# The first weight load of a cached-attention kernel as two transfers (16 rows and 112) instead of one of 128

## The chip, the cores and the metric

One core of a Trainium2 chip runs the whole kernel. The metric is device time in microseconds for one execution. The kernel before was timed in three runs: 678.33, 678.34 and 678.43 us, median 678.34 us.

## The reference

One decoding step for 8 sequences of width 512. The input is layer-normed; attention with 32 query heads over 8 cached key/value heads of 4096 positions gives `s`, and a gated MLP gives `g`; the result is `x + s * silu(g)`. Cut to what matters:

```python
xn = _layernorm(x)                                   # 8 x 1 x 512
q = (xn @ wq).reshape(B, 1, 32, 128)                 # wq: 512 x 4096
scores = einsum("bhqd,bhkd->bhqk", q, k) * 128**-0.5 # k_cache, v_cache: 8 x 8 x 4096 x 128
s = einsum("bhqk,bhkd->bhqd", softmax(scores), v) @ wo
z = gelu(xn @ w_in); z1, z2 = halves of z
g = silu((z1 * (w_sp * _layernorm(z2) + b_sp)) @ w_out)
return x + s * g
```

Everything is float32. The two caches are 134 MB each, wq and wo 8.4 MB each, and every byte is read once.

## The kernel before, in words

The on-chip memory holds three large slots, `slot_a`, `slot_b` and `slot_c`. Each has 128 rows (partitions) of 64 KB: 8.39 MB. Nearly all data passes through them in whole-slot transfers, and the host has laid out every array so that row p of a slot is one contiguous run of 64 KB in main memory.

All loads are issued by one engine's queue, SyncE (SP), in program order, and run in that order on the core's 16 DMA engines:

- In `prologue`: wq into `slot_b` (L96), x into a corner of `slot_c` (L103, 8 rows of 2 KB), the MLP's weights `w_mlp` into the rest of `slot_c` (L104, 128 rows of 42 KB), and the first half of head 0's keys, `kT[0, 0]`, into `slot_a` (L105). None of these four waits for anything. Then, when the q products have read wq, the second half of the keys goes into `slot_b` (L161).
- In `Heads.loads`, for each of the 8 key/value heads: values' first half into `slot_c` (L278), values' second half into `slot_b` (L280), the next head's keys' first half into `slot_a` (L283) and second half into `slot_b` (L276). Each waits until TensorE has read what the slot held. After the last head, wo comes into `slot_a` in seven pieces that are all 128 rows high and ever narrower (L285), and at last the rows of x for the final sum (L286).

The prologue's compute starts with the layer norm of x (L136 to L140), its transposition (L143, L144), and the q products with wq (64 matmuls, L151), for which both x and wq must have landed. The MLP follows (L164 to L224). Its transfers and engines are ordered by a scheduling framework, which adds the waits: an operation that reads a slot waits for each transfer that wrote the part it reads, and the load at L161 waits both for wq's landing and for the matmuls that read it.

In `Heads` the waits are written by hand with semaphores. `head_products` is TensorE's program, a loop over the heads: scores for the keys in `slot_a` and `slot_b` (L358), a few small products for the softmax, then the products with the values in `slot_c` and `slot_b` (L380). `head_sides` is what VectorE and ScalarE do beside it: maximum, exponentials, transposition, sums. `last_products` and `last_sides` multiply by wo (L415, L424, L437) as its pieces land, multiply by the gate and add x (L264), and ScalarE stores the result (L335).

Of the kernel before, what the change touches and what calls it, by code (L numbers as in the profile page):

```python
# [33 lines left out]
STEPS = 8  # L34
WARM = 384
AHEAD_OF_V = 11


class Chip:
# [52 lines left out]
def prologue(tc, t, x, w_mlp, wq, k0, k1, landed_a, landed_b):  # L92

    nc = tc.nc
    slot_a, slot_b, slot_c = t.slots
    nc.sync.dma_start(slot_b, wq)  # L96
    wq_sb = slot_b.rearrange("p (k n) -> p k n", k=NK)
    w_in_sb = slot_c[:, :N_IN].rearrange("p (k n) -> p k n", k=NK)
    w_out_sb = slot_c[:, N_IN:N_IN + N_OUT].rearrange("p (j d) -> p j d", j=NB)
# [131 lines left out]
class Heads:  # L231
# [116 lines left out]
    def head_products(self):  # L348
# [20 lines left out]
        for half, (slot, landed) in enumerate(((slot_c, self.landed_c), (slot_b, self.landed_b))):  # L369
            if half:  # L370
                flat = t.pT.rearrange("p j b g r -> p (j b g r)")
                with nc.tensor.Fori(0, AHEAD_OF_V):
                    nc.tensor.matmul(t.scr[1], t.ident, flat[:, :512], start=True, stop=True)  # L373
# [74 lines left out]
def gqa_gmlp_decode(nc, x, kT, v, wq, wo, w_mlp, x_rows, out):  # L448
    t = Chip(nc)
    landed_a, landed_b, stored = (nc.alloc_semaphore(s) for s in ("landed_a", "landed_b", "stored"))  # L450
    with tile.TileContext(nc) as tc:
        prologue(tc, t, x, w_mlp, wq, kT[0, 0], kT[0, 1], landed_a, landed_b)
    heads = Heads(nc, t, landed_a, landed_b, stored)
    heads.loads(kT, v, wo, x_rows)
    for h in range(HKV):
        heads.head_sides(h)
    heads.last_sides(out)
    nc.sync.wait_ge(stored, 16).then_inc(stored, -16)
    with nc.tensor.Fori(0, HKV):
        heads.head_products()  # L460
    heads.last_products()
# [39 lines left out]
```

## Time and profile before

| | |
|---|---|
| median of three runs | 678.34 us |
| profiled execution | 678.71 us, span 677.4 us |
| TensorE matmul busy | 405.8 us (60%) |
| VectorE busy | 80.0 us (12%) |
| DMA | 290.89 MB, mean 429 GB/s over the span |
| mean granted TensorE clock | 0.816 |

The profile is of one execution. Its span runs from the first to the last instruction; the profiled execution's own time is a little longer, and lies 0.37 us above the median. A row of a group or an issue names the line of the kernel, the engine, the tile written and the tile read. "SPq" is the queue of SyncE, which issues the loads. For an issue, the last number is the time until the data has landed. In the forty slices, DMA is the busy share of the 16 DMA engines in tenths.

### The profile page before, as it was taken

The page shows a single profiled execution, that of the slowest core. Times are in us where ns is not written, and L with a number is a line of the kernel's source. Part 1 is how long each engine was busy: PE and PEld are TensorE (multiplying, and loading weights), DVE is VectorE, ACT ScalarE, POOL GpSimd, SP SyncE. Part 2 cuts the span into 40 slices and gives each one's busy share as a digit, 9 for nine tenths or more (in the row PEclk, how much of TensorE's full clock was granted, in tenths as well). Part 3 has the DMA queues.
Part 4 walks back from the last instruction along what each step waited for, and adds up shares of the span by engine and source line. Part 5 has one row for each costly group of instructions (what it writes and reads, how often), then busy time and mean ns, then how long its engine had stood idle before and what let it go on. Part 6 is the DMA issues. An engine that isn't in the chain of part 4 may idle for free. (4 is left out here: it accounts for less than half of the span.)

```text
span 677.4 us, 5930 instructions
## 1 busy us (share of the span) xinstructions
PE 405.8 (60%) x2660; PEld 133.2 (20%) x2660; DVE 80.0 (12%) x157; ACT 13.8 (2%) x28; POOL 2.8 (0%) x15
## 2 busy tenths in 40 slices
PE   0446749346875449445794349555593349655598
PEld 0112213111221113111231113111131013211134
DVE  0142021102110021102110021101100021100211
ACT  0010000000000000000000000000000000000000
POOL 1000000000000000000000000000000000000000
PEclk9986869787896669788796779877696788976699
DMA  9999999999999999999999999999999999999997
GB/s 379 443 433 434 434 434 433 434 433 433 433 433 433 433 433 433 433 433 433 433 433 433 433 433 433 433 433 433 433 433 433 433 433 433 433 433 433 433 444 304
DMA packets 6213, 290.89 MB, mean 429 GB/s; under 512 B 952, under 2 KB 1080, under 8 KB 1600
## 3 DMA queue, kind: packets, MB, share of 16 engines
q1 hardware_dynamic: 6064, 290.79, 99.3%
q8 instruction: 4, 0.07, 0.0%
q10 hardware_dynamic: 144, 0.03, 0.0%
q14 instruction: 1, 0.01, 0.0%
HBM read 290.78 MB, written 0.03 MB: 429 GB/s over the span
## 5 line engine op out<-in xcount | busy, mean ns | idle before, releaser
L358 PE MATMUL sc<-slot_b,q 128*32 128x512 f32 x512 | 72.8, 733 | 75.8 <-PEq L340 75.8
L358 PE MATMUL sc<-slot_a,q 128*32 128x512 f32 x512 | 71.8, 724 | 72.4 <-PEq L340 72.4
L380 PE MATMUL o_ps<-slot_c,pT 128*16 128x512 f32 x512 | 72.4, 729 | 50.8 <-PEq L340 50.8
L373 PE MATMUL scr<-pT,ident 128*128 128x512 f32 x176 | 77.7, 597 | 0.0
L380 PE MATMUL o_ps<-slot_b,pT 128*16 128x512 f32 x512 | 56.5, 593 | 5.0 <-PEq L340 4.9
L358 PEld LDWEIGHTS sc<-slot_b,q 128*32 128x32 f32 x512 | 20.5, 132 | 128.2 <-issue 128.2
L264 DVE TENSOR_REDUCE nm<-sc 128x1 f32<-128x1024 f32 x8 | 9.8, 1224 | 290.1 <-PE sc L358 290.1
L358 PEld LDWEIGHTS sc<-slot_a,q 128*32 128x32 f32 x512 | 19.9, 131 | 117.9 <-issue 117.9
L373 PEld LDWEIGHTS scr<-pT,ident 128*128 128x128 f32 x176 | 32.8, 190 | 45.1 <-issue 45.1
L380 PEld LDWEIGHTS o_ps<-slot_c,pT 128*16 128x16 f32 x512 | 17.2, 112 | 99.4 <-issue 99.4
L380 PEld LDWEIGHTS o_ps<-slot_b,pT 128*16 128x16 f32 x512 | 15.7, 97 | 45.0 <-issue 45.0
L264 DVE TENSOR_TENSOR p<-o_ps,diag 128x512 f32<-128x512 f32 x8 | 5.5, 691 | 124.4 <-PE o_ps L380 124.4
L295 ACT ACTIVATE p<-sc,nm 128x1024 f32<-128x1024 f32 x8 | 8.9, 1114 | 554.3 <-DVE nm L264 554.3
L264 DVE TENSOR_TENSOR o_all<-o_ps,diag 128x512 f32<-128x512 f32 x8 | 5.5, 691 | 104.6 <-PE o_ps L380 104.6
L143 PE MATMUL scr<-ident,slot_c 8*128 8x8 f32 x4 | 0.6, 254 | 25.2 <-DVE slot_c L140 25.2
L345 PE MATMUL scr<-pT,ident 128*128 128x384 f32 x36 | 13.8, 507 | 0.0
L151 PE MATMUL scr<-slot_b,xnT 128*32 128x512 f32 x64 | 9.9, 779 | 0.3 <-DVE xnT L144 0.3
L262 DVE STREAM_TRANSPOSE pT<-p 128x1024 f32<-128x1024 f32 x8 | 10.0, 1245 | 0.3
L362 PE MATMUL scr<-ident,nm 128*1 128x128 f32 x8 | 2.2, 269 | 11.9 <-PEq L340 11.9
L262 DVE TENSOR_REDUCE o_sb<-p 128x128 f32<-128x512 f32 x8 | 8.3, 1033 | 0.3
L262 DVE TENSOR_REDUCE o_sb<-o_all 128x128 f32<-128x512 f32 x8 | 8.3, 1032 | 0.3
L388 PEld LDWEIGHTS po<-fold,o_sb 128*128 128x128 f32 x32 | 4.8, 188 | 13.5 <-issue 13.5
(96 smaller groups left out, 100.3 us busy)
## 6 DMA issues: line engine op xcount, KB each, us to landing
slot_c<-in_w_mlp SPq DMA_DIRECT2D x1, 5392.0 KB, 34.0
slot_a<-in_wo SPq DMA_DIRECT2D x1, 4608.0 KB, 39.2
slot_a<-in_wo SPq DMA_DIRECT2D x1, 1280.0 KB, 41.7
slot_a<-in_wo SPq DMA_DIRECT2D x2, 512.0 KB, 44.7
slot_a<-in_wo SPq DMA_DIRECT2D x1, 768.0 KB, 43.1
slot_a<-in_wo SPq DMA_DIRECT2D x1, 384.0 KB, 45.4
slot_a<-in_kT SPq DMA_DIRECT2D x8, 48.6
slot_b<-in_kT SPq DMA_DIRECT2D x8, 31.4
```

The lines of the kernel that those rows point to most:

```text
L143: nc.tensor.transpose(pt[:, k * B:(k + 1) * B], xn[:, k * P:(k + 1) * P], t.ident[:B, :B])
L151: nc.tensor.matmul(pq[R * g:R * (g + 1), :], t.xnT[:, k, :], wq_sb[:, k, lo:lo + REP * DH], start=(k == 0), stop=(k == NK - 1))
L262: make(*args, **kw).then_inc(self.token, 1)
L264: make(*args, **kw).then_inc(self.dve, 1)
L295: nc.scalar.activation(p, t.sc.rearrange("p c s -> p (c s)"), AF.Exp, bias=t.nm, accum_out=t.l).then_inc(self.act, 1)
L345: self.nc.tensor.matmul(t.scr[1][:, :WARM], t.ident, t.pT.rearrange("p j b g r -> p (j b g r)")[:, :WARM], start=True, stop=True)
L358: mm = nc.tensor.matmul(t.sc[R * g:R * (g + 1), c, :], t.q[:, b * R:(b + 1) * R], k_sb[:, i, c, g, :], start=(b == 0), stop=(b == B - 1))
L362: step(nc.tensor.transpose(t.scr[0][:1, :P], t.nm, t.ident))
L373: nc.tensor.matmul(t.scr[1], t.ident, flat[:, :512], start=True, stop=True)
L380: mm = nc.tensor.matmul(of[R * i:R * i + G * REP, :], pT[:, j, half * HALF + i], v_sb[:, i, j], start=(j == 0), stop=(j == J - 1))
L388: mm = nc.tensor.matmul(t.po[:, half * n:(half + 1) * n], t.o_sb[half], t.fold.rearrange("p i r -> p (i r)"), start=True, stop=True)
```

## The change

In `prologue`, the load of wq is written as two transfers, issued one right after the other on the same queue: first the first 16 rows, then the other 112. The same bytes go to the same places, and nothing else is touched.

```diff
 AHEAD_OF_V = 11
+FIRST_ROWS = 16
...
     slot_a, slot_b, slot_c = t.slots
-    nc.sync.dma_start(slot_b, wq)
+    nc.sync.dma_start(slot_b[:FIRST_ROWS], wq[:FIRST_ROWS])
+    nc.sync.dma_start(slot_b[FIRST_ROWS:], wq[FIRST_ROWS:])
     wq_sb = slot_b.rearrange("p (k n) -> p k n", k=NK)
```

## The prediction

> **What bounds the kernel now.** I read the page first: engine shares, the forty slices, the DMA queues and issues.
>
> ```profile
> PE 405.8 (60%) x2660; PEld 133.2 (20%) x2660; DVE 80.0 (12%) x157; ACT 13.8 (2%) x28; POOL 2.8 (0%) x15
> ...
> DMA  9999999999999999999999999999999999999997
> GB/s 379 443 433 434 434 434 433 434 433 433 433 433 433 433 433 433 433 433 433 433 433 433 433 433 433 433 433 433 433 433 433 433 433 433 433 433 433 433 444 304
> ...
> q1 hardware_dynamic: 6064, 290.79, 99.3%
> ...
> slot_a<-in_kT SPq DMA_DIRECT2D x8, 48.6
> slot_b<-in_kT SPq DMA_DIRECT2D x8, 31.4
> slot_c<-in_v SPq DMA_DIRECT2D x8, 50.3
> slot_b<-in_v SPq DMA_DIRECT2D x8, 29.3
> ```
>
> No compute engine is near full; the transfers are. The rate stands at 433 GB/s through nearly every slice, and 290.79 MB / 433 GB/s = 671.6 us of a 677.4 us span. A large transfer here is 128 rows of 64 KB, 8.39 MB, so 8.39 MB / 433 GB/s = 19.4 us alone; the shortest median from issue to landing is 29.3 us, so it is issued some 10 us before its turn. The queue has no hole between the first load and the last, and what is lost at its head is lost at the end.
>
> To see that the end hangs on it, I took the chain that ended last, in order of time, and the waits of the loading queue.
>
> ```profile
> 673.68 0.04 issue
> 673.72 0.64 PE acc L424 x32
> ...
> 675.61 0.22 DVE gate L264
> ...
> SPq L280 <- PE sc L358: 300.8, 8, 40.6
> ...
> SPq L161 <- DMA slot_b<-in_wq: 20.2, 1, 20.2
> ```
>
> The chain is two microseconds of work at the very end, on the last pieces of wo. The loader waits for TensorE in between (L280), but by the landings above never so long that the transfers run dry.
>
> Now the head, which is all that the change touches: windows of the first 8 us. A packet is booked whole in the window where it starts (hence shares over 1), so bytes divided by 64 KB count the rows that start there.
>
> ```profile
> core 0: us, PE busy (x) PEld busy (x) DVE busy (x) ACT busy (x) POOL busy (x), PEclk, DMA share, GB/s
> 1.70:1.80 0.10, 0.00 (x0) 0.00 (x0) 0.10 (x1) 0.00 (x0) 0.10 (x2) 1.00 5.86 1966
> 1.80:2.60 0.80, 0.00 (x0) 0.00 (x0) 0.79 (x5) 0.00 (x0) 0.44 (x4) 1.00 2.84 983
> 2.60:2.70 0.10, 0.00 (x0) 0.00 (x0) 0.00 (x0) 0.00 (x0) 0.04 (x1) 1.00 1.83 655
> 2.70:4.80 2.10, 0.00 (x0) 0.00 (x0) 0.00 (x0) 0.00 (x0) 0.00 (x0) 1.00 0.00 0
> 4.80:4.85 0.05, 0.00 (x0) 0.00 (x0) 0.00 (x0) 0.00 (x0) 0.00 (x0) 1.00 6.05 2621
> 4.85:5.50 0.65, 0.00 (x0) 0.00 (x0) 0.00 (x0) 0.00 (x0) 0.00 (x0) 1.00 3.02 1311
> 5.50:5.60 0.10, 0.00 (x0) 0.00 (x0) 0.00 (x0) 0.00 (x0) 0.00 (x0) 1.00 1.51 655
> 5.60:7.20 1.60, 0.00 (x0) 0.00 (x0) 0.00 (x0) 0.00 (x0) 0.00 (x0) 1.00 0.00 0
> 7.20:7.30 0.10, 0.00 (x0) 0.00 (x0) 0.00 (x0) 0.00 (x0) 0.00 (x0) 1.00 3.03 1311
> ```
>
> Row by row: 3 + 12 + 1 = 16 packets start in 1.7 to 2.7 us, one on each of the 16 DMA engines; the second sixteen start as 2 at 4.80, 13 in 4.85 to 5.50, and 1 in 5.50 to 5.60; the third begin at 7.2. So an engine takes 7.2 - 4.8 = 2.4 us for a row of 64 KB (433 GB/s / 16 = 27.1 GB/s, 2.42 us, the figure I use), the first row takes about 4.8 - 1.75 = 3.05 us, and the last engine stands 5.55 - 4.80 = 0.75 us behind the first. Each engine has eight rows of wq.
>
> **The change, part by part.** *Issue.* One more transfer is issued. In order of time:
>
> ```profile
> 0.73 0.37 SPq L96 DMA_DIRECT2D slot_b<-in_wq  x1
> 1.16 0.36 SPq L103 DMA_DIRECT2D slot_c<-in_x  x1
> 1.58 0.35 SPq L104 DMA_DIRECT2D slot_c<-in_w_mlp  x1
> 1.98 0.66 SPq L105 DMA_DIRECT2D slot_a<-in_kT  x1
> ```
>
> An issue takes 0.35 to 0.37 us whether it carries 8 rows (x) or 128, so the first one does not shorten. The second piece is issued at about 1.16 and could start some 1.0 us later, 2.2 us (0.73 to 1.74 for the first): before any engine has ended a first row, hence hidden. x, w_mlp and the first kT are issued 0.42 us later, behind 19 us of wq in the same queue: nothing. Without that cover it would be 0.42 us.
>
> *Waits.* The q matmuls (L151), and the loader at L161, now wait for two landings. The second piece stands last in the queue, so it decides, as wq does now; the loader's issue behind it (kT into slot_b, at 37.5 us) comes 31.4 us before a landing that needs 19.4, as above, and moves along with everything. No cost of its own.
>
> *Start of the engines.* The first piece gives every engine one row. If the 0.9 us over which the first rows start is the time to hand out 8 rows per engine, one row each is handed out faster, and the last engine can win up to its 0.75 us of lag; bounds 0 and -0.75. As every later row follows without a gap, the last engine decides. I take the full -0.75.
>
> *Rows of one piece.* What the trace before does not show is sixteen neighbouring rows of 64 KB in flight at once: all its large transfers spread 128 rows, and which sixteen of them are in flight together it doesn't tell. Best bound: each runs as now, 2.42 us, no cost. Worst bound: neighbours go in one at a time, 16 x 2.42 = 38.7 us for the first piece, +36.3. Nearest to the question is x, eight neighbouring rows, but of 2 KB:
>
> ```profile
> 21.70:21.75 0.05, 0.00 (x0) 0.00 (x0) 0.00 (x0) 0.00 (x0) 0.00 (x0) 1.00 0.23 82
> ```
>
> 82 GB/s x 0.05 us = 4.1 KB, two of its rows started together, and 0.23 x 16 x 0.05 = 0.18 us of packet time, 0.09 each, against 0.076 at 27.1 GB/s: no sign of taking turns. But two rows of 2 KB may sit in a buffer on the way, or lie on different ways. And the flat 433 GB/s says that something on the way is full all the time; if that is the way into the on-chip memory and not the engine, neighbours can crowd it. I hold that the likelier, since a limit that sits in ways shared by rows would show exactly this flat ceiling as long as rows are spread evenly, and all of them are. So I do not take the best bound; between factors of 1 and 16 I take the middle by ratio, 4: four of the sixteen at full rate. The first piece then costs 4 x 2.42 - 2.42 = +7.26 us.
>
> [...]
>
> *The other 112 rows.* Seven rows per engine, of neighbouring runs now cut at 7 and not at 8, so engines meet where they did not before. Bounds: no meetings, 0; pairs meeting in every row, 7 x 2.42 = +16.9; as bad as the first piece in every row, 7 x 7.26 = +50.8. The nearest row is the 128-row transfer, with none; against it stands that the engines leave the first piece out of step with the ways they go. I take pairs in half of the rows: +8.5.
>
> Sum: -0.75 + 7.26 + 8.5 = +15.0 us. The profiled execution took 678.71 us (span 677.4) and would become 693.7; that run lies 0.37 above the median of 678.34, so as a median 693.3. The delay carries through whole: after wq every transfer has 128 rows, and the last engine stays last.
>
> **The rivals.** (a) *Only the first piece pays.* The seven-row runs spread as the eight-row ones do: -0.75 + 7.26 = +6.5, 684.8. For it, 112 rows are nearly all of 128; against it, the cut at 7.
> (b) *The second piece is as crowded as the first*: if row n goes to engine n mod 16, sixteen neighbours are always in flight: -0.75 + 7.26 + 50.8 = +57.3, 735.6. Nothing in the profile speaks for such a split; it is not excluded.
> (c) *Neighbouring rows don't get in each other's way.* Speaks for it: the two rows of x. Then only the start moves, by 0 to -0.75: 677.6 to 678.3, no measurable change. This is also the case in which the change doesn't do what it says, if the 0.9 us spread isn't the handing out of rows.
> (d) *The other side: faster.* The first row takes 3.05 us and not 2.42. If that excess too comes from descriptors of later rows being written while the first row moves, a short first piece wins 0.63 + 0.75 = 1.4 us, 676.9. It needs no crowding at all and nearly all of both; it decides from 1.36 us (0.2%). Against it: the first row of a cold queue may simply include its latency, which stays.
>
> **How the numbers follow.** About 0.2%, 1.4 us, is what this kernel's measurement can tell from no change. Forecast (both pieces pay, +9 to +23): 0.56. (a): 0.14. (b): 0.08. (c): 0.17. (d): 0.05. Slower is the forecast, (a) and (b): 0.78; same 0.17; faster 0.05. The likeliest time is 693.3; its own range is 687 to 702, the top from pairs in every row (-0.75 + 7.26 + 16.9 = +23.4, 701.8) and the bottom from pairs in one row of seven (+8.9). As (c) holds 0.17 the whole range must reach into it: 677.5 to 702, which leaves out (b), (d) and little else.
>
> **What would show it.** In the windows of the first 15 us: sixteen first rows starting within a narrower stretch than 1.7 to 2.7 (the start step), then no second rows until about 4.8 + 7.26 = 12 us (the crowding). If second rows begin near 4.8 us, the crowding is wrong and (c) or (d) holds. wq's landing, now 22.8 us after the start (0.73 + 22.1 by the row below), should be near 38; near 29 is (a).
>
> ```profile
> slot_b<-in_wq SPq DMA_DIRECT2D x1, 22.1
> ```
>
> From then on the slices should stand at 433 GB/s as before, and the last chain should look the same, shifted. The prediction goes wrong if the later transfers, by their own spread, make up for a late engine, or if a row's way into the memory has room that a 64 KB row can't fill.

## The result, and the profile after

The changed kernel takes 698.72 us (median of six runs) against 678.45 us for the kernel before: 20.3 us more, a ratio of 1.0303 with a 95% interval of 1.0292 to 1.0314. The forecast was slower, 693.3 us, with 677.5 to 702 as its range. Four of the six runs took 698.46 to 698.73 us and two took 700.03 and 700.06, so a single run of such a kernel can't be read more finely than some 1.6 us. The profiled execution has a span of 697.4 us, 20.0 more than before.

From the page of the changed kernel, the DMA share and rate of its forty slices, and four issues of loads:

```profile
DMA  9999999999999999999999999999999999999997
GB/s 180 241 333 450 426 418 437 440 437 429 429 432 451 429 425 440 432 444 429 429 432 451 429 425 440 429 444 432 429 432 451 429 425 436 429 447 429 432 423 315
...
slot_a<-in_kT SPq DMA_DIRECT2D x8, 48.2
slot_b<-in_kT SPq DMA_DIRECT2D x8, 31.4
slot_c<-in_v SPq DMA_DIRECT2D x8, 50.3
slot_b<-in_v SPq DMA_DIRECT2D x8, 29.3
```

The first three slices move 180, 241 and 333 GB/s where they moved 379, 443 and 433. A slice is 17.4 us, so the loss is (199 + 202 + 100) x 17.4 / 433 = about 20.1 us: all of it. The DMA engines count as busy in these slices too (the digit is 9 at 180 GB/s as at 433), since a row counts as in flight for its whole time, 8.55 us in the first piece (below); the share alone would have hidden the loss, the rate shows it. After that the slices stand around 433 again (418 to 451 GB/s up to the last two) and the landings are those of before, so nothing was given back and nothing more lost. The end, as the chain that ended last has it, is the same work 20 us later:

```profile
694.65 0.70 PE acc L426 x28
...
695.63 0.23 DVE gate L266
```

VectorE's first operation on x, which stands right behind wq in the queue, dates the end of the wq stage, before and after:

```profile
22.92 0.68 DVE L136 BATCH_NORM_STATS2 st<-slot_c 8x6 f32<-8x512 f32 x1 [20.33 <-DMA slot_c<-in_x]
```

```profile
43.43 0.68 DVE L138 BATCH_NORM_STATS2 st<-slot_c 8x6 f32<-8x512 f32 x1 [40.84 <-DMA slot_c<-in_x]
```

That is 20.5 us later, and the end of the span moved by 20.0. The mark is good to a fraction of a microsecond only: in the run with rows seven apart, further down, it stands at 42.77 us with the same total. Inside the stage, windows of the changed kernel, each cut so that it holds the starts of exactly sixteen rows, as many as there are engines (GB/s x width = 1.05 MB = 16 x 64 KB). DMA share x width is then the mean time of one row (the last two columns are the share and the GB/s):

```profile
1.70:2.70 1.00, 0.00 (x0) 0.00 (x0) 0.89 (x5) 0.00 (x0) 0.59 (x5) 1.00 8.55 1049
9.90:11.30 1.40, 0.00 (x0) 0.00 (x0) 0.00 (x0) 0.00 (x0) 0.00 (x0) 1.00 3.82 749
15.50:16.30 0.80, 0.00 (x0) 0.00 (x0) 0.00 (x0) 0.00 (x0) 0.00 (x0) 1.00 5.99 1311
20.30:21.10 0.80, 0.00 (x0) 0.00 (x0) 0.00 (x0) 0.00 (x0) 0.00 (x0) 1.00 4.02 1311
23.40:25.80 2.40, 0.00 (x0) 0.00 (x0) 0.00 (x0) 0.00 (x0) 0.00 (x0) 1.00 1.55 437
27.00:29.40 2.40, 0.00 (x0) 0.00 (x0) 0.00 (x0) 0.00 (x0) 0.00 (x0) 1.00 1.89 437
31.30:34.10 2.80, 0.00 (x0) 0.00 (x0) 0.00 (x0) 0.00 (x0) 0.00 (x0) 1.00 1.70 374
36.00:38.90 2.90, 0.00 (x0) 0.00 (x0) 0.00 (x0) 0.00 (x0) 0.00 (x0) 1.00 1.59 362
```

The first piece: 8.55 us a row. The seven rows of the second: 3.82 x 1.40 = 5.35, then 4.79, 3.22, 3.72, 4.54, 4.76 and 4.61 us, 31.0 us together. The same reading of the kernel before gives 3.04 us for the first row and 3.02 x 0.80 = 2.42 us for the second:

```profile
1.70:2.70 1.00, 0.00 (x0) 0.00 (x0) 0.89 (x5) 0.00 (x0) 0.58 (x5) 1.00 3.04 1049
4.80:5.60 0.80, 0.00 (x0) 0.00 (x0) 0.00 (x0) 0.00 (x0) 0.00 (x0) 1.00 3.02 1311
```

So the first piece costs 8.55 - 3.04 = 5.5 us, and the second 31.0 - 7 x 2.42 = 14.1 us: 19.6 as a mean over the engines, some 20.5 by the mark, which waits for the last of them.

### The profile page after: what moved, and what is told of

Same layout as the page of the kernel before. It is cut to its first block, busy times and chain, and to the rows that moved or that the text cites. A ratio compares the mean times of both kernels' runs of the same rounds, so it can differ in the third digit from the quotient of the medians.

```text
span 697.4 us, 5932 instructions
## 1 busy us (share of the span) xinstructions
PE 407.0 (58%) x2660; PEld 133.2 (19%) x2660; DVE 80.1 (11%) x157; ACT 13.8 (2%) x28; POOL 2.8 (0%) x15
## 5 line engine op out<-in xcount | busy, mean ns | idle before, releaser
L360 PE MATMUL sc<-slot_a,q 128*32 128x512 f32 x512 | 74.6, 748 | 72.3 <-PEq L342 72.3
L360 PEld LDWEIGHTS sc<-slot_b,q 128*32 128x32 f32 x512 | 20.2, 132 | 128.0 <-issue 128.0
L360 PEld LDWEIGHTS sc<-slot_a,q 128*32 128x32 f32 x512 | 20.5, 134 | 120.0 <-issue 120.0
```

What stands on the lines that cost most here:

```text
L360: mm = nc.tensor.matmul(t.sc[R * g:R * (g + 1), c, :], t.q[:, b * R:(b + 1) * R], k_sb[:, i, c, g, :], start=(b == 0), stop=(b == B - 1))
```

## The experiments

All start from the kernel before and change only how wq is loaded (for two of them also how the host lays the array out). The kernel before took 678.47 us beside the first seven, 678.87 beside the pieces seven apart and 678.35 beside the pieces nine apart; times to which no interval is given are of a single run.

**Is it the splitting?** Two transfers again, but cut by columns:

```diff
-    nc.sync.dma_start(slot_b, wq)
+    first_cols = SLOT // 8
+    nc.sync.dma_start(slot_b[:, :first_cols], wq[:, :first_cols])
+    nc.sync.dma_start(slot_b[:, first_cols:], wq[:, first_cols:])
```

> wq again in two transfers, the first again of 1 MB, but cut by columns: both pieces have all 128 rows (8 KB of each row, then 56 KB). Theory A (rows of one piece that lie near each other crowd on the way into the on-chip memory): no crowding, as every piece spreads over 128 rows, so the time is that of before within 0.75 us, 677.7 to 678.8. Theory C (the splitting itself costs, by the second landing or a small first piece): slower by about 20 us as the change was, 698. If a short first piece brought the engines' starts closer together, up to 0.75 us would be won; the change's trace, whose first rows again start over 0.9 us, speaks against that.

Measured: 678.57 us, ratio 1.000 (0.9991 to 1.0009). Its issues:

```profile
slot_b<-in_wq SPq DMA_DIRECT2D x1, 7168.0 KB, 21.2
slot_b<-in_wq SPq DMA_DIRECT2D x1, 1024.0 KB, 4.7
```

The first 1 MB lands in 4.7 us and the rest as wq did (21.2 us from its issue, wq 22.1). A second issue, a second landing and a small first piece cost nothing that can be measured (678.57 against 678.47 us), and win nothing. So it isn't the splitting that costs, but a cut by rows.

**An even cut.** 64 rows and 64:

```diff
-    nc.sync.dma_start(slot_b, wq)
+    nc.sync.dma_start(slot_b[:64], wq[:64])
+    nc.sync.dma_start(slot_b[64:], wq[64:])
```

> wq in two transfers of 64 rows each, an even cut of four rows per engine. Theory A with engines meeting in pairs in every row (4.8 us for a row of 64 KB where 2.42 is full rate): 8 x 2.42 = 19.4 us more, 697.8, and second rows that start some 4.8 us after the first. Theory D (the 16 neighbours and the uneven seven rows per engine are what costs, an even cut of large pieces is free): 678 to 679. [...]

Measured: 699.6 us, 21.1 more. Windows with sixteen row starts each:

```profile
6.20:7.40 1.20, 0.00 (x0) 0.00 (x0) 0.00 (x0) 0.00 (x0) 0.00 (x0) 1.00 4.28 874
11.30:12.50 1.20, 0.00 (x0) 0.00 (x0) 0.00 (x0) 0.00 (x0) 0.00 (x0) 1.00 4.28 874
```

4.28 x 1.20 = 5.14 us a row, a little over twice 2.42. It is not the sixteen rows or the uneven seven.

**Only neighbours.** Eight pieces of 16 rows:

```diff
-    nc.sync.dma_start(slot_b, wq)
+    for i in range(8):
+        nc.sync.dma_start(slot_b[16 * i:16 * (i + 1)], wq[16 * i:16 * (i + 1)])
```

> wq in eight transfers of 16 neighbouring rows, each like the first piece of the change, whose rows took some 8.4 us. Theory A: 8 x 8.4 = 67 us (up to 8 x 9.7 = 77 if four at a time is exact) instead of 19.4, so 48 to 58 us more, 726 to 736. Theory C (each split costs a fixed amount, 20 us for the first): 7 splits, 140 us more, 818. If it was only the start of a cold queue that made the change's first piece slow: 678 to 685.

Measured: 732.7 us, 54.2 more. Its slices:

```profile
GB/s 115 115 115 115 360 456 448 417 448 413 444 416 448 448 423 444 416 444 416 448 448 423 444 416 444 416 448 448 423 444 416 444 416 448 448 423 444 416 440 310
```

For four slices the sixteen engines together move 115 GB/s, 4.2 times 27.1 GB/s, an engine's share of the full rate. A slice books a row where it starts, so the 115 is rounded to whole rows (32 in 18.3 us); windows with the sixteen starts of the first piece and of the second:

```profile
1.70:2.30 0.60, 0.00 (x0) 0.00 (x0) 0.60 (x4) 0.00 (x0) 0.27 (x3) 1.00 14.49 1748
9.80:11.20 1.40, 0.00 (x0) 0.00 (x0) 0.00 (x0) 0.00 (x0) 0.00 (x0) 1.00 6.64 749
```

A row of the first piece takes 14.49 x 0.60 = 8.69 us, one of the second 6.64 x 1.40 = 9.30, 3.8 times 2.42. That confirms the factor of 4, on 16 neighbours that don't start cold.

**On-chip or main memory?** Two kernels, each with eight pieces of 16. In the first the 16 rows are neighbours in main memory and land four apart; in the second they are neighbours in the slot and come from every eighth row of main memory. The host lays the array out to match.

```diff
-    nc.sync.dma_start(slot_b, wq)
+    for i in range(8):
+        lo = 64 * (i // 4) + i % 4
+        nc.sync.dma_start(slot_b[lo:lo + 61:4], wq[16 * i:16 * (i + 1)])
```

> wq in eight transfers of 16 rows as in the run with eight pieces of neighbours, and each still reads 16 neighbouring rows of main memory, but they land four rows apart in the slot (rows 0, 4, .. 60 and so on; the array is laid out for it). Theory A (the place in the on-chip memory decides): less crowding than with neighbours; if four rows next to each other share a way, these pieces have each way shared by two, 4.8 us per row, 19.4 us more, 698. Theory B (the place in main memory decides): as with eight pieces of neighbours, 726 to 736. Theory C likewise as there.

```diff
-    nc.sync.dma_start(slot_b, wq)
+    for i in range(8):
+        nc.sync.dma_start(slot_b[16 * i:16 * (i + 1)], wq[i::8])
```

> wq in eight transfers of 16 neighbouring rows of the slot, as in the run with eight pieces of neighbours (732.7 us), but each piece reads its rows from every eighth row of main memory (512 KB apart) instead of 16 neighbouring ones. Theory A (the place in the on-chip memory decides): 732.7 within 2 us. Theory B (the place in main memory decides): faster, toward the 699.6 of the pieces that land four rows apart, or slower still if rows 512 KB apart meet in main memory.

Measured: 699.64 us for rows that land four apart, 733.32 for rows that come from far apart but land side by side. The slices of the second are the 115 GB/s of the neighbours again:

```profile
GB/s 115 115 115 115 360 458 438 416 455 409 448 415 448 451 412 451 415 448 415 444 455 412 448 415 448 426 433 455 412 448 415 448 451 412 451 415 448 415 436 310
```

Where the rows land decides, and where they come from doesn't. Theory B falls. How many rows share a way, the fours and twos of the expectations here and further down, is an assumption that no run shows; what was measured of the rows four apart is 2.69 x 1.90 = 5.11 us a row in a window with sixteen row starts, as in the even cut (5.14):

```profile
11.00:12.90 1.90, 0.00 (x0) 0.00 (x0) 0.00 (x0) 0.00 (x0) 0.00 (x0) 1.00 2.69 552
```

**The order.** The change's pieces the other way round, 112 rows and then 16:

```diff
-    nc.sync.dma_start(slot_b, wq)
+    nc.sync.dma_start(slot_b[:112], wq[:112])
+    nc.sync.dma_start(slot_b[112:], wq[112:])
```

> The change's two pieces in the other order: rows 0 to 111 first, then rows 112 to 127. Both are crowded as before if Theory A holds and the order is nothing: 698 to 700. If the 112 rows were slow only because the 16 neighbours had sent the engines out of step, they now run at 2.42 us a row and only the 16 last rows cost, +6 to +7: 684 to 685. If x and w_mlp, which follow in the queue, fill the ways that the 16 last rows leave idle, a few us less than 698.

Measured: 698.32 us. Windows with sixteen row starts each, the seven steps of the 112 rows:

```profile
1.70:2.70 1.00, 0.00 (x0) 0.00 (x0) 0.89 (x5) 0.00 (x0) 0.58 (x5) 1.00 4.08 1049
5.30:7.00 1.70, 0.00 (x0) 0.00 (x0) 0.00 (x0) 0.00 (x0) 0.00 (x0) 1.00 2.78 617
10.00:12.00 2.00, 0.00 (x0) 0.00 (x0) 0.00 (x0) 0.00 (x0) 0.00 (x0) 1.00 2.36 524
14.70:16.60 1.90, 0.00 (x0) 0.00 (x0) 0.00 (x0) 0.00 (x0) 0.00 (x0) 1.00 1.81 552
18.20:20.30 2.10, 0.00 (x0) 0.00 (x0) 0.00 (x0) 0.00 (x0) 0.00 (x0) 1.00 1.72 499
21.60:24.20 2.60, 0.00 (x0) 0.00 (x0) 0.00 (x0) 0.00 (x0) 0.00 (x0) 1.00 1.74 403
25.80:28.80 3.00, 0.00 (x0) 0.00 (x0) 0.00 (x0) 0.00 (x0) 0.00 (x0) 1.00 1.60 350
```

Share x width: 4.08, 4.73, 4.72, 3.44, 3.61, 4.52 and 4.80 us. The very first row is slow (4.08 against 3.04 before), so the 112 rows are slow by themselves, not because the 16 sent the engines out of step. The two quickest steps are now the fourth and fifth; in the change they are the third and fourth.

**32 rows and 96:**

```diff
-    nc.sync.dma_start(slot_b, wq)
+    nc.sync.dma_start(slot_b[:32], wq[:32])
+    nc.sync.dma_start(slot_b[32:], wq[32:])
```

> wq as 32 rows and then 96: two rows per engine, then six. If the neighbouring rows share ways by fours, 32 rows reach twice as many ways as 16, so each of its rows takes 4.8 us: +4.8. For the 96: if engines meet in pairs in every row, 6 x 2.42 = +14.5, together 697.7; if the 96 were cut free of meetings, 683.2; if they lose like the change's 112 (14.9 us over 7 rows, 2.1 a row), +12.8, together 696.

Measured: 698.64 us, 20.2 more: above all three expectations, and nearest to pairs in every row (697.7).

**Who carries which of the 112?** The 16 neighbours, then seven pieces of 16 rows that stand seven apart:

```diff
-    nc.sync.dma_start(slot_b, wq)
+    nc.sync.dma_start(slot_b[:16], wq[:16])
+    for u in range(7):
+        nc.sync.dma_start(slot_b[16 + u:128:7], wq[16 + u:128:7])
```

> Which engine carries which of the 112 rows? The 16 neighbours first, as in the change, then seven transfers of 16 rows that stand seven apart (rows 16, 23, .. 121; then 17, 24, .. 122; and so on). If in the change each engine carries seven successive rows, this is the same work in the same order, engine by engine: 698.7 within 1 us, the landing of wq near 43.4 us, and the same row times (about 5.2, 4.8, 3.0, 3.6, 4.5, 4.7, 4.5 us). If the 112 rows are dealt out otherwise (one to each engine in turn, say), the time differs: 684.8 if rows seven apart never meet, up to 702 if they meet in pairs in every row. [...]

Measured: 698.71 us, beside 698.72 for the changed kernel. That close an agreement is chance, as runs of the changed kernel differ by 1.6 us; the steps say more. Windows with sixteen row starts each, first piece, then the seven steps:

```profile
1.70:2.70 1.00, 0.00 (x0) 0.00 (x0) 0.89 (x5) 0.00 (x0) 0.58 (x5) 1.00 8.42 1049
9.30:11.40 2.10, 0.00 (x0) 0.00 (x0) 0.00 (x0) 0.00 (x0) 0.00 (x0) 1.00 2.58 499
15.20:16.60 1.40, 0.00 (x0) 0.00 (x0) 0.00 (x0) 0.00 (x0) 0.00 (x0) 1.00 3.42 749
20.00:21.20 1.20, 0.00 (x0) 0.00 (x0) 0.00 (x0) 0.00 (x0) 0.00 (x0) 1.00 2.63 874
23.10:25.90 2.80, 0.00 (x0) 0.00 (x0) 0.00 (x0) 0.00 (x0) 0.00 (x0) 1.00 1.39 375
26.90:29.80 2.90, 0.00 (x0) 0.00 (x0) 0.00 (x0) 0.00 (x0) 0.00 (x0) 1.00 1.59 362
31.20:34.50 3.30, 0.00 (x0) 0.00 (x0) 0.00 (x0) 0.00 (x0) 0.00 (x0) 1.00 1.42 318
35.90:39.20 3.30, 0.00 (x0) 0.00 (x0) 0.00 (x0) 0.00 (x0) 0.00 (x0) 1.00 1.37 318
```

Share x width: 8.42, then 5.42, 4.79, 3.16, 3.89, 4.61, 4.69 and 4.52 us, against 8.55, 5.35, 4.79, 3.22, 3.72, 4.54, 4.76 and 4.61. The ups and downs match step by step, within 0.2 us, so in the change, too, the rows in flight together stand seven apart, as they do if each engine carries seven successive rows, and what slows a step is which sixteen rows are in flight together. The run with the 112 rows first agrees, where the quick steps moved with the rows.

**Rows that should not meet.** Nine pieces of 14 rows that stand nine apart, and the last 2 rows:

```diff
-    nc.sync.dma_start(slot_b, wq)
+    for u in range(9):
+        nc.sync.dma_start(slot_b[u:u + 118:9], wq[u:u + 118:9])
+    nc.sync.dma_start(slot_b[126:], wq[126:])
```

> Ten pieces, and none of the large ones crowded: nine transfers of 14 rows that stand nine apart (rows 0, 9, .. 117; then 1, 10, .. 118; and so on), and one of the last 2 rows. [...] Theory A with that spacing: 2.42 us a row, nine rows on each of 14 engines, 21.8 us, and then two neighbouring rows at half rate, 4.8 us, on two of them: 26.6 us against 19.4, 7.3 us more, 685.7 (683.3 if the two don't meet). Rival: a piece with fewer rows than 128 is slow wherever they stand, at the 4.6 us a row of the pieces seven apart: 9 x 4.6 + 4.8 = 46 us, 27 us more, 705.

Measured: 696.58 us. The total misses both expectations, so the stage has to be read by its steps. Windows with fourteen row starts each (0.92 MB), the second to seventh row of an engine, with the stretch between the last two of them, and after them one of the loader's later issues:

```profile
5.40:6.30 0.90, 0.00 (x0) 0.00 (x0) 0.00 (x0) 0.00 (x0) 0.00 (x0) 1.00 2.36 1020
7.80:8.70 0.90, 0.00 (x0) 0.00 (x0) 0.00 (x0) 0.00 (x0) 0.00 (x0) 1.00 2.36 1020
10.20:11.20 1.00, 0.00 (x0) 0.00 (x0) 0.00 (x0) 0.00 (x0) 0.00 (x0) 1.00 2.12 918
12.60:13.60 1.00, 0.00 (x0) 0.00 (x0) 0.00 (x0) 0.00 (x0) 0.00 (x0) 1.00 2.14 918
15.10:16.00 0.90, 0.00 (x0) 0.00 (x0) 0.00 (x0) 0.00 (x0) 0.00 (x0) 1.00 2.66 1020
16.00:17.50 1.50, 0.00 (x0) 0.00 (x0) 0.00 (x0) 0.00 (x0) 0.00 (x0) 1.00 0.24 58
17.50:19.10 1.60, 0.00 (x0) 0.00 (x0) 0.00 (x0) 0.00 (x0) 0.00 (x0) 1.00 1.70 573
```

```profile
13.78 0.35 SPq L106 DMA_DIRECT2D slot_c<-in_w_mlp  x1
```

The first three of these steps run at 2.36 x 0.90 x 16 / 14 = 2.43 us a row, and the fourth at 2.45: small pieces, and no crowding in these steps. That rows nine apart don't meet was the expectation's assumption; these four steps are what shows it. The rival falls, and Theory A with that spacing holds while these rows are alone. From 15.1 us on a row takes 2.74 and then 3.11 us. The MLP's weights are issued at 13.78, and as 14 rows occupy 14 engines, two have nothing of wq to carry and can run ahead to those weights. The line from 16.00 to 17.50 us shows it: 58 GB/s x 1.50 us = 87,000 bytes start there, two rows of 42 KB, and no row of wq is that short. The step behind it again holds just fourteen rows of 64 KB, so nothing shows that the last 2 rows of wq had begun, nor the half rate that the expectation assumed for them. That the MLP's rows slow those of wq fits in time, but no run leaves them out, and how the 18.2 us add up, where 7.3 were expected, stays open.

## Why the prediction was right, and where its terms were off

The bound and the carry-through held: the queue had no hole (the DMA digit is 9 in 39 of the forty slices), the stage's 20.5 us arrived at the end of the span as 20.0 (20.3 between the medians), and the rate after the stage is that of before (418 to 451 GB/s up to the last two slices, around 433).

The mechanism held as far as the runs show it: rows of one piece that land side by side slow each other, and where they land decides it (699.64 us when they land four apart, 733.32 when only their places in main memory are spread). Where on the way they wait for each other, no run shows. The factor of 4 had been the middle by ratio between 1 and 16, a choice with no row behind it, so it is in part luck that it came so near: a row took 8.55 us in the change (3.5 times 2.42) and 9.30 in the run of neighbours (3.8 times). The 2 KB rows of x, which had shown no turns (0.09 us each), gave no hint of it: the wrong row to go by for rows of 64 KB.

Rivals (c) and (d) fell with the first windows, rival (a) with the second piece's 14 us, and rival (b), sixteen neighbours at all times, with the time (698.72 us against its 735.6) and the run of pieces seven apart. Of the signs that the prediction named, the second rows began at 9.9 us and not at 12, and the stage ended near 43 us and not 38: the first piece was cheaper and the second dearer than it had them.

Three terms of the sum were mis-sized.

*Start of the engines*, -0.75: the win did not come. With one row for each engine to hand out, the first rows of the changed kernel start over the same stretch as before, 1.7 to 2.7 us. Two narrow windows of the changed kernel at its ends:

```profile
1.70:1.80 0.10, 0.00 (x0) 0.00 (x0) 0.10 (x1) 0.00 (x0) 0.10 (x2) 1.00 21.60 2621
2.60:2.70 0.10, 0.00 (x0) 0.00 (x0) 0.00 (x0) 0.00 (x0) 0.04 (x1) 1.00 5.30 655
```

Four rows start at its beginning and one at its end. So one row per engine does not by itself make the stretch shorter than eight do. It isn't fixed either: in the run of neighbours, whose first piece is the same, all sixteen rows start between 1.7 and 2.3 us. What sets it stays open; the cut by columns didn't shorten the time either.

*First piece*, +7.26: it cost 5.5. The prediction took the first row's excess over 2.42 us, 0.63, as an addition that stays; 8.55 us is nearer to 3.5 x 2.42, with the start included.

*Second piece*, +8.5: it cost 14.1, near the upper bound of 16.9. The assumption was pairs in half of the rows. One of its reasons, that the engines leave the first piece out of step, isn't needed: the 112 rows sent first are as slow (3.44 to 4.80 us a row). In the trace every step costs something (3.22 to 5.35 us against 2.42), and in the first step every engine pays. All sixteen rows of it start before 11.2 us, and the next row starts at 15.6 or later:

```profile
11.20:15.60 4.40, 0.00 (x0) 0.00 (x0) 0.00 (x0) 0.00 (x0) 0.00 (x0) 1.00 0.00 0
```

So none of the sixteen took less than 4.4 us. That is what the half was too low for. No run shows engines meeting in pairs, so the term was the author's estimate; nor does one show why the third and fourth steps (3.22 and 3.72 us) cost less than the other five (4.54 to 5.35). The prediction's premise that the 128 rows of one transfer go in runs of eight isn't shown either: rows seven apart match the steps of the 112, but no run loads rows eight apart, and of the kernel before only the 2.42 us a row is known.

The three misses partly cancel: 0.75 and 5.6 too low, 1.8 too high, which is 4.6 of the 5.3 us between 15.0 and 20.3. The rest is about the last engine against the mean (20.5 against 19.6).

One reading was loose, without harm: the prediction has an issue at 0.35 to 0.37 us, and the issue of kT in the same lines took 0.66. All of them are hidden behind wq: the last of these issues ends at 2.64 us, and wq lands at 22.8.

## What to carry to other kernels

Cut a large load by columns, so that every piece keeps all 128 rows: the one such cut tried here cost nothing (678.57 against 678.47 us), while every cut by rows tried here cost 18 us or more on 8.39 MB. In a kernel whose load queue never runs dry, a slow first load is paid in full at the end, as the change shows (20.0 of 20.5 us). Look at the rate of the early slices and not at the DMA's busy share, which stays full while rows slow each other (9 tenths at 180 GB/s in the first slice of the change).

## What the runs showed that was not expected

Cuts as different as 64 + 64, 32 + 96, 16 + 112 and sixteen rows four apart all came to between 698.3 and 699.6 us, some 5 us a row as a mean over the eight rows of an engine, though the change gets there with one row of 8.55 us and seven of 4.4 on average, and the halves with 5.1 in the steps shown. Pieces of 14 rows nine apart ran at 2.43 us a row on 14 engines for three steps, so a piece with fewer than 128 rows is not slow in itself.
